# High and low parts of split fp32 weights, side by side instead of apart: a linear-attention and two-MoE kernel

## The chip, the cores and the metric

One core of a Trainium2 chip runs the whole program. The metric is the device time of one execution in microseconds, the median over several runs. Before the change it is 745.47 us (three runs).

## What is computed

A gated linear attention over 4 × 8 heads, 768 steps and 48 features a head; its output, 3072 tokens of 384 features, goes through two feed-forward layers: one with a softmax-weighted activation and a layer norm (1024 wide), one with h · cos(h) (2048 wide).

```python
def _attn_ref(q, k, v, alpha):
    for t in range(S):
        state = alpha[:, :, t, :, None] * state + np.einsum('bhd,bhe->bhde', k[:, :, t], v[:, :, t])
        y[:, :, t] = np.einsum('bhd,bhde->bhe', q[:, :, t], state)

def _moe_ref(x, w_in, w_out, g_ln):
    h = x @ w_in
    e = np.exp(h - np.max(h, axis=-1, keepdims=True))
    solu = h * (e / (np.sum(e, axis=-1, keepdims=True) + 1e-09))
    mu, var = np.mean(solu, axis=-1, keepdims=True), np.mean((solu - mu) ** 2, axis=-1, keepdims=True)
    return ((solu - mu) / np.sqrt(var + 1e-06) * g_ln) @ w_out

def _moe2_ref(x, w_in, w_out):
    h = x @ w_in
    return (h * np.cos(h)) @ w_out
```

The weights arrive as 64-bit floats and are turned into 32-bit ones on the chip.

## The kernel before

**Split products.** TensorE multiplies in a reduced fp32 form, F32R, at one column of the moving operand a cycle. To keep fp32 accuracy, each operand is split into a high part (a copy rounded to F32R, by ScalarE) and a low part (the difference, by VectorE or GpSimd), and each product is three matmuls: high·high, high·low, low·high. Every matmul has a load of its own, of 128 columns of weights in most cases, that runs beside the matmul ahead of it. The plain F32 matmuls and transposes of the attention are not split.

**Phase one** (about the first 340 us). The tokens come in 24 tiles of 128 (4 batches × 6 chunks). For each, attention forms `pa` (scores, L298), `px` (values, L329) and the state (`pst`, L348). Then `values_high` and `values_low` split its output into `xh` and `xl` (L380, L385), and `hidden` (L397) multiplies: here x is the loaded operand (the weights of TensorE) and `win_h`, `win_l` move, 512 columns at a time, 18 matmuls a tile. After softmax and norm, `turn` transposes the tile (L464: `so` is loaded, the identity moves, plain F32), `turn_high` and `turn_low` split it into `lth` and `ltl`, two tiles side by side, and `project` (L485 to L487) multiplies: `wout_h`, `wout_l` are loaded, `lth`, `ltl` move, 256 columns, 72 matmuls for each of 12 pairs of tiles. The result is `x2T`. The order of phase one is written out by hand as a list of words, PLAN; each word issues one step.

**Phase two.** The tokens come in 6 blocks (b) of 512, and the 2048 hidden features in 16 chunks (c) of 128. The 96 pairs (b, c) are slots in one sequence. `h2` (L573 to L575) makes a chunk's 9 matmuls: w2 is loaded, the block's `x2h`, `x2l` move, 512 columns. ScalarE and VectorE then form g = h · cos(h) and split it into `gh`, `gl` (L580 to L608). `out_mm` (L620 to L622) makes 9 matmuls for the chunk two slots back: w2 is loaded, `gh`, `gl` move. So a slot has 18 matmuls of 512 columns.

**Chunks of w2.** `w2load` fetches a chunk's 768 columns (384 for `h2`, 384 for `out_mm`) from HBM to `w2r`; `w2high` and `w2low` split it into `w2h` and `w2l` once (L550, L554), and all six blocks use the result. Chunks 0 to 3 are made in PLAN, 4 to 15 in the slots of block 0, three slots ahead. In each part the 128 columns of one load lie next to one another, 4 bytes apart, 512 bytes in all.

**Where things lie.** Tiles of a pool lie one behind the other in each partition. `x2h`, `x2l` of even blocks are in pool "q"; those of odd blocks are in pool "q3", behind `out`, a tile of ROWS columns of 4 bytes. In the built program `x2h` starts at byte 196576 of a partition in even blocks and at 128096 in odd ones: modulo 256, 224 and 96. `x2l` lies 6144 bytes on, at the same remainder. `w2h`, `w2l`, `gh`, `gl`, `xh`, `xl`, `win`, `wout`, `lth` and `ltl` all start at 224 modulo 256.

Of the kernel before, what the change touches and what calls it, by code (L numbers as in the profile page):

```python
# [27 lines left out]
DM = H * D  # L28
# [21 lines left out]
WB = 768  # L50
HB = WB // 2
NWB = ((KT * FF1 + NF1 * DM) // WB + NF2) * 2
ROWS = 96

TINY = float(np.array([897 << 20], np.int32).view(np.float32)[0])

# [65 lines left out]
def _build(tc, a):  # L122
# [5 lines left out]
    def flat(t):  # L128
        return t.rearrange("p a b -> p (a b)")

    with top:
# [22 lines left out]

        win_h = wi.tile([128, KT, FF1], F32R, name="win_h")
        win_l = wi.tile([128, KT, FF1], F32R, name="win_l")
        wout_h = wo.tile([128, NF1, DM], F32R, name="wout_h")
        wout_l = wo.tile([128, NF1, DM], F32R, name="wout_l")
        mask = at.tile([128, 128], F32, name="mask", bufs=1)
        d1p = at.tile([128, AW], F32, name="d1p", bufs=1)  # L160
        d1r = at.tile([128, AW], F32, name="d1r", bufs=1)
# [38 lines left out]
        def split(n):  # L200

            name = weights[n]
            w = T["w", name]
            j = int(name[1:])
            if name[0] == "o":
                for q in range(2):
                    ws = w[:, q * DM:(q + 1) * DM]
                    A.activation(ws, ws, AF.Copy, scale=gln[:, 2 * j + q:2 * j + q + 1])
                hi, lo = [t[:, 2 * j:2 * j + 2, :].rearrange("p a b -> p (a b)") for t in (wout_h, wout_l)]
            else:  # L210
                hi, lo = [flat(t)[:, j * 512:(j + 1) * 512] for t in (win_h, win_l)]
            A.activation(hi, w, AF.Copy)
            T["split", n] = hi, lo
# [161 lines left out]

        def values_high(i):
            px = T["px", i]
            xh = sm.tile([128, KT, 128], F32R, name=f"xh{i}", tag="xh", bufs=LA + 1)
            xl = sm.tile([128, KT, 128], F32R, name=f"xl{i}", tag="xl", bufs=LA + 1)
            A.activation(xh, px, AF.Copy, scale=2.0)  # L380
            T["x", i] = xh, xl

# [84 lines left out]
        def turn_high(i, half):  # L467
            g, j = i // GT, i % GT
            if ("lt", g) not in T:
                T["lt", g] = [sm.tile([128, NF1, GN], F32R, name=f"lt{x}{g}", tag="lt" + x) for x in "hl"]  # L470
            dst = (slice(None), slice(half * 4, half * 4 + 4), slice(j * C, (j + 1) * C))
            A.activation(T["lt", g][0][dst], T["pl", i, half], AF.Copy)

# [29 lines left out]

        def win_load(j):

            t = flat(sm.tile([128, NF1, GN], F32R, name=f"rawi{j}", tag="lth" if j % 2 else "ltl")).bitcast(F32)
            raw = t[:, 0:1024].bitcast(I32).rearrange("p (n two) -> p n two", two=2)
            top = mags[j % 2][:, j // 2 % 2 * 512:(j // 2 % 2 + 1) * 512]
            conv_load(a["win"][:, j * 512:(j + 1) * 512], f"i{j}",
                      (raw, (top.bitcast(I32), t[:, 1024:1536].bitcast(I32))))  # L510
# [32 lines left out]
        def w2load(c):  # L543
            raw = pools["q"].tile([128, WB], F32, name=f"w2r{c}", tag="w2r")
            SP.dma_start(raw, w2f[c])
            W[c] = raw, [pools["w"].tile([128, WB], F32R, name=f"w2{x}{c}") for x in "hl"]

        def w2high(c):
            raw, (wh, wl) = W[c]
            A.activation(wh, raw, AF.Copy)  # L550

        def w2low(c, eng=G):
            raw, (wh, wl) = W[c]
            eng.tensor_tensor(wl, raw, wh.bitcast(F32), ALU.subtract)  # L554
            W[c] = wh, wl

        def xhigh(b, k):
            if k == 0:
# [8 lines left out]
        def h2(b, c):  # L567
            xh, xl = X[b]
            wh, wl = W[c]
            ph = pools["h"].tile([128, BLK], F32, name=f"h2_{b}_{c}", tag="h2", bufs=3)  # L570
            for k in range(KT):
                ks = slice(k * 128, (k + 1) * 128)
                PE.matmul(ph, wh[:, ks], xh[:, k, :], start=k == 0, stop=False)  # L573
                PE.matmul(ph, wh[:, ks], xl[:, k, :], start=False, stop=False)  # L574
                PE.matmul(ph, wl[:, ks], xh[:, k, :], start=False, stop=k == KT - 1)  # L575
            Hs[b, c] = ph

        def turns(b, c):
# [32 lines left out]
        def out_mm(b, c):  # L611
            gh, gl = Gs.pop((b, c))
            wh, wl = W[c]
            if c == 0:
                O[b] = [pools["o"].tile([128, BLK], F32, name=f"o{b}_{f}", tag=f"o{f}", bufs=1 + (f < 2))
                        for f in range(KT)]
            for f in range(KT):
                fs = slice(DM + f * 128, DM + (f + 1) * 128)
                po = O[b][f]
                PE.matmul(po, wh[:, fs], gh, start=c == 0, stop=False)  # L620
                PE.matmul(po, wl[:, fs], gh, start=False, stop=False)  # L621
                PE.matmul(po, wh[:, fs], gl, start=False, stop=c == NF2 - 1)  # L622

        def out_end(b, fs=range(KT)):
            for f in fs:
# [323 lines left out]
```

## Time and profile before

| | us | share of the span |
|---|---|---|
| median of 3 runs | 745.47 | |
| profiled execution | 747.37 | |
| its span (first to last instruction) | 745.5 | |
| TensorE busy, matmuls | 721.9 | 97% |
| TensorE busy, weight loads (beside matmuls) | 608.6 | 82% |
| VectorE busy | 585.5 | 79% |
| ScalarE busy | 441.7 | 59% |
| GpSimd busy | 110.8 | 15% |

The busy time of a matmul in this profile reaches to a modelled end, past the start of the next one, so a busy TensorE can still have gaps between the starts of its matmuls that its columns don't explain. How far apart matmuls start is read from the timeline. PE is the engine's matmul row, PEld its row of weight loads; DVE is VectorE, ACT is ScalarE, POOL is GpSimd.

### The profile page before, as it was taken

The numbers are of one execution on the slowest core, as the hardware profiler recorded it, in microseconds if no ns is written. First come the engines' busy times: TensorE is split into PE (matmuls) and PEld (weight loads), VectorE is DVE, ScalarE is ACT, GpSimd is POOL, SyncE is SP. The second block draws the span as 40 slices with busy tenths as digits, with TensorE's granted clock in tenths as the row PEclk, the third lists the DMA queues.
The fourth block names the chain that finished last, engine by engine and source line by source line (L and its number), as shares of the span: only waits on it lengthen the run. The fifth ranks groups of instructions, "written<-read, shape, count | busy, mean of one in ns | idle before, by whom it ended". The sixth has DMA issues, their size and how long they took to land.

```text
span 745.5 us, 13977 instructions
## 1 busy us (share of the span) xinstructions
PE 721.9 (97%) x5580; PEld 608.6 (82%) x5580; DVE 585.5 (79%) x988; ACT 441.7 (59%) x771; POOL 110.8 (15%) x107
## 2 busy tenths in 40 slices
PE   6789999999999999999999999999999999999995
PEld 3578888899889898989888888888888888888884
DVE  6998988888698765543898878887888888888873
ACT  4799777866645556683665554555455555545442
POOL 3354531255311000310000000000000000000000
PEclk8899999999999999999999999999999999999999
DMA  9868777693433401111240421141142134134311
GB/s 324 233 175 202 246 199 215 209 257 95 91 78 59 89 2 44 29 59 40 87 125 32 148 72 50 44 140 36 49 135 63 43 99 137 41 91 143 89 38 48
DMA packets 27961, 81.19 MB, mean 109 GB/s; under 512 B 3600, under 2 KB 6928, under 8 KB 27888
## 3 DMA queue, kind: packets, MB, share of 16 engines
q1 hardware_dynamic: 27888, 80.22, 37.8%
q8 instruction: 46, 0.75, 0.4%
q14 instruction: 27, 0.22, 0.1%
HBM read 69.19 MB, written 11.01 MB: 108 GB/s over the span
## 4 chain that ended last, share of the span: by engine, by line
PE 55%; ACT 0%; DVE 0%; issue 0%
PE o L620 9%; PE h L575 9%; PE o L621 9%; PE h L573 9%; PE o L622 9%; PE h L574 9%; PE po L487 1%; PE po L486 1%; PE po L485 1%; PE pl L464 0%; ACT so L456 0%; ACT e L409 0%; DVE ob L632 0%; DVE ob L629 0%; ACT ob L630 0%; ACT c L451 0%
## 5 line engine op out<-in xcount | busy, mean ns | idle before, releaser
L593 ACT ACTIVATE g<-r,consts 128x512 f32<-128x512 f32 x96 | 69.5, 724 | 97.1 <-DVE r L587 97.1
L580 ACT ACTIVATE n<-h,consts 128x512 int32<-128x512 f32 x96 | 66.0, 688 | 86.0 <-PE h L575 86.0
L575 PE MATMUL h<-x2h,w2l 128*128 128x512 f32 x288 | 113.0, 392 | 0.0
L573 PE MATMUL h<-x2h,w2h 128*128 128x512 f32 x288 | 113.0, 392 | 0.0
L621 PE MATMUL o<-gh,w2l 128*128 128x512 f32 x288 | 112.7, 391 | 0.0
L620 PE MATMUL o<-gh,w2h 128*128 128x512 f32 x288 | 112.6, 391 | 0.0
L574 PE MATMUL h<-x2l,w2h 128*128 128x512 f32 x288 | 112.5, 391 | 0.0
L622 PE MATMUL o<-gl,w2h 128*128 128x512 f32 x288 | 112.1, 389 | 0.0
L586 DVE SCALAR_TENSOR_TENSOR r<-n,h 128x512 f32<-128x512 int32 x96 | 66.1, 688 | 40.1 <-ACT n L580 39.7
L598 DVE TENSOR_TENSOR g<-g,h 128x512 f32<-128x512 f32 x96 | 66.1, 688 | 24.4 <-ACT g L593 24.4
L485 PE MATMUL po<-lth,wout_h 128*128 128x256 f32 x288 | 83.1, 289 | 0.1
L486 PE MATMUL po<-ltl,wout_h 128*128 128x256 f32 x288 | 81.4, 283 | 0.0
L487 PE MATMUL po<-lth,wout_l 128*128 128x256 f32 x288 | 81.4, 283 | 0.0
L587 DVE SCALAR_TENSOR_TENSOR r<-n,r 128x512 f32<-128x512 int32 x96 | 66.5, 693 | 3.3
L608 DVE TENSOR_TENSOR gl<-g,gh 128x512 fp32r<-128x512 f32 x96 | 65.7, 684 | 1.5 <-ACT gh L603 1.5
L575 PEld LDWEIGHTS h<-x2h,w2l 128*128 128x128 f32 x288 | 54.0, 188 | 12.2
L620 PEld LDWEIGHTS o<-gh,w2h 128*128 128x128 f32 x288 | 54.0, 188 | 12.1 <-ACT x2T L491 0.2
L622 PEld LDWEIGHTS o<-gl,w2h 128*128 128x128 f32 x288 | 54.1, 188 | 11.8 <-DVE gl L608 0.2
L574 PEld LDWEIGHTS h<-x2l,w2h 128*128 128x128 f32 x288 | 54.0, 188 | 11.8
L621 PEld LDWEIGHTS o<-gh,w2l 128*128 128x128 f32 x288 | 54.1, 188 | 11.8
L573 PEld LDWEIGHTS h<-x2h,w2h 128*128 128x128 f32 x288 | 54.1, 188 | 11.5
L603 ACT ACTIVATE gh<-g 128x512 fp32r<-128x512 f32 x96 | 59.8, 623 | 2.0 <-DVE g L598 1.6
(115 smaller groups left out, 1371.3 us busy)
## 6 DMA issues: line engine op xcount, KB each, us to landing
raw<-w SPq DMA_DIRECT2D x16, 768.0 KB, 5.5
wraw<-w SPq DMA_DIRECT2D x32, 384.0 KB, 3.1
pk<-pack SPq DMA_DIRECT2D x42, 288.9 KB, 5.6
w2f<-top SPq DMA_DIRECT2D x16, 384.0 KB, 4.6
w2r<-w2f SPq DMA_DIRECT2D x16, 384.0 KB, 3.1
v<-vpack SPq DMA_DIRECT2D x24, 224.0 KB, 6.1
al<-alpha SPq DMA_DIRECT2D x18, 256.0 KB, 3.0
outT<-ob SPq DMA_DIRECT2D x18, 256.0 KB, 2.1
```

The lines of the kernel that those rows point to most:

```text
L485: PE.matmul(po, wout_h[:, k, fs], lh[:, k, :], start=k == 0, stop=False)
L486: PE.matmul(po, wout_h[:, k, fs], ll[:, k, :], start=False, stop=False)
L487: PE.matmul(po, wout_l[:, k, fs], lh[:, k, :], start=False, stop=k == NF1 - 1)
L573: PE.matmul(ph, wh[:, ks], xh[:, k, :], start=k == 0, stop=False)
L574: PE.matmul(ph, wh[:, ks], xl[:, k, :], start=False, stop=False)
L575: PE.matmul(ph, wl[:, ks], xh[:, k, :], start=False, stop=k == KT - 1)
L586: V.scalar_tensor_tensor(out=r, in0=n, scalar=-C1, in1=ph, op0=ALU.mult, op1=ALU.add)
L587: V.scalar_tensor_tensor(out=r, in0=n, scalar=-C2, in1=r, op0=ALU.mult, op1=ALU.add)
L593: A.activation(g, r, AF.Sin, bias=halfpi)
L620: PE.matmul(po, wh[:, fs], gh, start=c == 0, stop=False)
L621: PE.matmul(po, wl[:, fs], gh, start=False, stop=False)
L622: PE.matmul(po, wh[:, fs], gl, start=False, stop=c == NF2 - 1)
```

## The change

High and low parts that were two tiles become one, with the two parts of an element next to each other. A load of one part then reads every second element: its 128 columns lie 8 bytes apart and span 1024 bytes. This is done for wout, for x in phase one (`xh`, `xl`), and for chunks 7 to 11 of w2. In chunks 12 to 15 the high and low parts of two column groups are put together, so that columns lie 16 bytes apart and a load spans 2048 bytes. Chunks 0 to 6 stay at 4 bytes. The operations that write the parts write them at these steps.

Two places change. `out` has 128 columns instead of 96, so `x2h` of odd blocks starts at 128224, 224 modulo 256. `lth` and `ltl` get a pool of their own, "ltp", behind all others of phase one, and start at 64 modulo 256 instead of 224. Every other tile named above keeps 224 modulo 256; the low part of an interleaved tile starts 4 bytes behind the high one (8 bytes at step 16).

All engines carry the same operations in the same order as before, with the same numbers of partitions and elements; on ScalarE one wait (for the transfer of a w2 chunk) has become an instruction of its own. The new lines number three more than the old ones in phase one.

```diff
-ROWS = 96
+ROWS = 128
+STEPS = [1] * 7 + [2] * 5 + [4] * 4
...
+        ltp = left.enter_context(tc.tile_pool(name="ltp", bufs=2))
...
-        wout_h = wo.tile([128, NF1, DM], F32R, name="wout_h")
-        wout_l = wo.tile([128, NF1, DM], F32R, name="wout_l")
+        wout = wo.tile([128, NF1, DM, 2], F32R, name="wout")
+        wout_h, wout_l = wout[:, :, :, 0], wout[:, :, :, 1]
...
-                hi, lo = [t[:, 2 * j:2 * j + 2, :].rearrange("p a b -> p (a b)") for t in (wout_h, wout_l)]
+                both = wout[:, 2 * j:2 * j + 2].rearrange("p a b two -> p (a b) two")
+                hi, lo = both[:, :, 0], both[:, :, 1]
...
-            xh = sm.tile([128, KT, 128], F32R, name=f"xh{i}", tag="xh", bufs=LA + 1)
-            xl = sm.tile([128, KT, 128], F32R, name=f"xl{i}", tag="xl", bufs=LA + 1)
+            x = sm.tile([128, KT, 128, 2], F32R, name=f"x{i}", tag="x", bufs=LA + 1)
+            xh, xl = x[:, :, :, 0], x[:, :, :, 1]
...
-                T["lt", g] = [sm.tile([128, NF1, GN], F32R, name=f"lt{x}{g}", tag="lt" + x) for x in "hl"]
+                T["lt", g] = [ltp.tile([128, NF1, GN], F32R, name=f"lt{x}{g}", tag="lt" + x) for x in "hl"]
...
-            W[c] = raw, [pools["w"].tile([128, WB], F32R, name=f"w2{x}{c}") for x in "hl"]
+            step = STEPS[c]
+            if step == 1:
+                t = pools["w"].tile([128, 2, 6, 128], F32R, name=f"w2hl{c}")
+                whole = [t[:, x] for x in range(2)]
+            elif step == 2:
+                t = pools["w"].tile([128, 6, 128, 2], F32R, name=f"w2hl{c}")
+                whole = [t[:, :, :, x] for x in range(2)]
+            else:
+                t = pools["w"].tile([128, 3, 128, 2, 2], F32R, name=f"w2hl{c}")
+                whole = [t[:, :, :, :, x].rearrange("p a f b -> p a b f") for x in range(2)]
+            W[c] = raw, whole, step
...
-                PE.matmul(ph, wh[:, ks], xh[:, k, :], start=k == 0, stop=False)
-                PE.matmul(ph, wh[:, ks], xl[:, k, :], start=False, stop=False)
-                PE.matmul(ph, wl[:, ks], xh[:, k, :], start=False, stop=k == KT - 1)
+                PE.matmul(ph, wh(k), xh[:, k, :], start=k == 0, stop=False)
+                PE.matmul(ph, wh(k), xl[:, k, :], start=False, stop=False)
+                PE.matmul(ph, wl(k), xh[:, k, :], start=False, stop=k == KT - 1)
```

`wh(j)` and `wl(j)` are the 128 columns of group j (0 to 2 for `h2`, 3 to 5 for `out_mm`) at the chunk's step.

## Rows read from the trace of the kernel before

**Rows 1.** The page: busy us (share) and instructions; granted clock in 40 slices.
```profile
PE 721.9 (97%) x5580; PEld 608.6 (82%) x5580; DVE 585.5 (79%) x988; ACT 441.7 (59%) x771; POOL 110.8 (15%) x107
...
PEclk8899999999999999999999999999999999999999
```
**Rows 2.** Timeline of PE, an even block (b = 2), one slot: start us, us, what.
```profile
502.08 0.39 PE L573 MATMUL h<-x2h,w2h 128*128 128x512 f32 x1
...
506.16 0.39 PE L573 MATMUL h<-x2h,w2h 128*128 128x512 f32 x1
```
**Rows 3.** Timeline of PE, an odd block (b = 1), one slot.
```profile
423.68 0.40 PE L573 MATMUL h<-x2h,w2h 128*128 128x512 f32 x1
...
427.84 0.40 PE L573 MATMUL h<-x2h,w2h 128*128 128x512 f32 x1
```
**Rows 4.** Timeline of PE, phase one, matmuls with wout, 21 starts apart.
```profile
325.68 0.28 PE L487 MATMUL po<-lth,wout_l 128*128 128x256 f32 x1
...
328.20 0.28 PE L487 MATMUL po<-lth,wout_l 128*128 128x256 f32 x1
```
**Rows 5.** Timeline of PE, phase one, eight transposes in a row.
```profile
336.14 1.04 PE L464 MATMUL pl<-ident,so 128*128 128x128 f32 x8
```
**Rows 6.** Groups by line and shape: count, busy us, mean ns, idle before.
```profile
L485 PE MATMUL po<-lth,wout_h 128*128 128x256 f32 x288 | 83.1, 289 | 0.1
...
L573 PEld LDWEIGHTS h<-x2h,w2h 128*128 128x128 f32 x288 | 54.1, 188 | 11.5
...
L397 PE MATMUL ph<-win_l,xh 128*128 128x512 f32 x144 | 45.4, 396 | 1.9 <-DVE win_l L218 1.9
...
L464 PE MATMUL pl<-ident,so 128*128 128x128 f32 x192 | 25.5, 274 | 0.6 <-ACT so L456 0.6
...
L348 PE MATMUL pst<-v,kt 128*32 128x64 f32 x640 | 12.5, 221 | 2.2 <-ACT kt L305 2.2
...
L348 PEld LDWEIGHTS pst<-v,kt 128*32 128x32 f32 x640 | 10.3, 110 | 4.8 <-ACT kt L305 3.6 <-issue 0.5 <-ACT xh L380 0.4
```
**Rows 7.** Busy time by stage: blocks b = 1 and b = 2 whole.
```profile
core 0: us, PE busy (x) PEld busy (x) DVE busy (x) ACT busy (x) POOL busy (x), PEclk, DMA share, GB/s
402.87:469.43 66.56, 66.56 (x289) 54.04 (x288) 53.87 (x100) 33.92 (x54) 4.68 (x7) 1.00 0.25 76
469.43:534.71 65.28, 65.28 (x289) 54.05 (x288) 53.82 (x100) 33.94 (x54) 4.31 (x7) 1.00 0.24 77
```
**Rows 8.** Timeline of PE, phase one, one state update.
```profile
252.20 0.63 PE L348 MATMUL pst<-v,kt 128*32 128x64 f32 x32
```
**Rows 9.** Busy time by stage: 40 to 160 us, all engines.
```profile
40.00:160.00 120.00, 116.70 (x1454) 102.63 (x1455) 106.30 (x163) 101.28 (x184) 47.74 (x37) 1.00 0.76 218
```
**Rows 10.** Busy time of L397 alone, then of L485 alone, until 160 us.
```profile
0.00:160.00 160.00, 46.79 (x184) 0.96 0.78 229
...
0.00:160.00 160.00, 27.85 (x96) 0.96 0.78 229
```
**Rows 11.** Groups by line: operations with and without steps, ScalarE and VectorE.
```profile
L655 DVE SCALAR_TENSOR_TENSOR wup<-wup,wraw 128x384 f32<-128x384 uint32 x48 | 26.8, 559 | 1.7
...
L190 ACT ACTIVATE low<-raw 128x768 bf16<-128x768 f32 x16 | 17.4, 1086 | 6.2 <-POOL top L198 3.7 <-DVE top L198 2.4
...
L385 DVE SCALAR_TENSOR_TENSOR xl<-px,xh 128x384 fp32r<-128x384 f32 x24 | 13.3, 553 | 2.9 <-ACT xh L380 2.7
...
L550 ACT ACTIVATE w2h<-w2r 128x768 fp32r<-128x768 f32 x16 | 13.3, 836 | 4.4 <-DMA w2r<-w2f 4.4
```

More of the change, by code (lines that the diff above doesn't have):

```diff
@@ L504, in win_load @@
         def win_load(j):
-            t = flat(sm.tile([128, NF1, GN], F32R, name=f"rawi{j}", tag="lth" if j % 2 else "ltl")).bitcast(F32)
+            t = flat(ltp.tile([128, NF1, GN], F32R, name=f"rawi{j}", tag="lth" if j % 2 else "ltl")).bitcast(F32)
             raw = t[:, 0:1024].bitcast(I32).rearrange("p (n two) -> p n two", two=2)
@@ L545, in w2load @@
             SP.dma_start(raw, w2f[c])
-            W[c] = raw, [pools["w"].tile([128, WB], F32R, name=f"w2{x}{c}") for x in "hl"]
+            step = STEPS[c]
[9 more added lines that the diff above has]
+            W[c] = raw, whole, step
         def w2high(c):
-            raw, (wh, wl) = W[c]
-            A.activation(wh, raw, AF.Copy)
+            raw, (wh, wl), step = W[c]
+            A.activation(wh, raw.rearrange("p (a b f) -> p a b f", a=3, b=2) if step == 4 else
+                         raw.rearrange("p (j f) -> p j f", j=6), AF.Copy)
         def w2low(c, eng=G):
-            raw, (wh, wl) = W[c]
-            eng.tensor_tensor(wl, raw, wh.bitcast(F32), ALU.subtract)
-            W[c] = wh, wl
+            raw, (wh, wl), step = W[c]
+            eng.tensor_tensor(wl, raw.rearrange("p (a b f) -> p a b f", a=3, b=2) if step == 4 else
+                              raw.rearrange("p (j f) -> p j f", j=6), wh.bitcast(F32), ALU.subtract)
+            W[c] = [(lambda j, t=t: t[:, j // 2, j % 2]) if step == 4 else (lambda j, t=t: t[:, j]) for t in (wh, wl)]
         def xhigh(b, k):
@@ L571, in h2 @@
             for k in range(KT):
-                ks = slice(k * 128, (k + 1) * 128)
-                PE.matmul(ph, wh[:, ks], xh[:, k, :], start=k == 0, stop=False)
-                PE.matmul(ph, wh[:, ks], xl[:, k, :], start=False, stop=False)
-                PE.matmul(ph, wl[:, ks], xh[:, k, :], start=False, stop=k == KT - 1)
+                PE.matmul(ph, wh(k), xh[:, k, :], start=k == 0, stop=False)
+                PE.matmul(ph, wh(k), xl[:, k, :], start=False, stop=False)
+                PE.matmul(ph, wl(k), xh[:, k, :], start=False, stop=k == KT - 1)
             Hs[b, c] = ph
@@ L617, in out_mm @@
             for f in range(KT):
-                fs = slice(DM + f * 128, DM + (f + 1) * 128)
                 po = O[b][f]
-                PE.matmul(po, wh[:, fs], gh, start=c == 0, stop=False)
-                PE.matmul(po, wl[:, fs], gh, start=False, stop=False)
-                PE.matmul(po, wh[:, fs], gl, start=False, stop=c == NF2 - 1)
+                PE.matmul(po, wh(KT + f), gh, start=c == 0, stop=False)
+                PE.matmul(po, wl(KT + f), gh, start=False, stop=False)
+                PE.matmul(po, wh(KT + f), gl, start=False, stop=c == NF2 - 1)
         def out_end(b, fs=range(KT)):
```

## The prediction

> **What bounds the kernel now.** I read the page's busy shares first, then the granted clock, the table by stage, and the starts of single matmuls. TensorE is busy 97% of the span, VectorE 79%, ScalarE 59%, and the granted clock stands at 9 tenths or more, its upper level of 2.4 GHz, from the third of 40 slices on [rows 1]. So time goes only where a matmul starts later after the one before it than its columns need. A "pitch" below is that distance from start to start; the trace's own durations of matmuls (389 ns) overlap and say less.
>
> Four pitches carry the argument.
> - A 512-column F32R matmul of an even block: 18 in 506.16 − 502.08 = 4.08 us, 226.7 ns each [rows 2]. Its columns need 512 / 2.4 = 213.3 ns.
> - The same in an odd block: 18 in 427.84 − 423.68 = 4.16 us, 231.1 ns [rows 3].
> - A 256-column one of phase one: 21 in 328.20 − 325.68 = 2.52 us, 120.0 ns each; the columns need 106.7 [rows 4].
> - A transpose of 128 plain F32 columns: 8 in 1.04 us, the last with a duration of 0.274, so (1.04 − 0.274) / 7 = 109 ns [rows 5, 6].
>
> So each F32R matmul carries about 13.3 ns beyond its columns, whether it has 512 or 256 of them: it goes with the load that runs beside each matmul, not with the columns.
>
> Is it reading that collides? Whole blocks answer: 66.56 us for an odd block, 65.28 for an even one, with the same count of matmuls and VectorE and ScalarE equally busy [rows 7]. They differ only in where the moving x2 lies: in the built program it starts at byte 128096 of a partition in odd blocks (96 modulo 256) and at 196576 in even ones (224 modulo 256, as do all w2 tiles and g). An address cannot matter to a cost that is fixed; so at least part of the excess is the moving operand and the weights getting in each other's way.
>
> The speeds of the two reads: a load of 128 columns takes 188 ns, one of 32 takes 110, so (188 − 110) / 96 = 0.81 ns a column, 4 bytes each [rows 6]. An F32R moving column passes in 0.417 ns, so now the moving read runs through memory twice as fast as the weights. Plain F32 moves at half that speed: the 32 records of a state update, four at a time with 64 columns each, take (0.63 − 0.221) / 7.75 = 0.053 us a group, 0.82 ns a column [rows 6, 8]. In a transpose, then, both reads walk at the same speed, and there the excess is 109 − 106.7 = 2.3 ns instead of 13.3, though a full 128-column load runs beside each. This pair is what I build on: **equal walking speed goes with almost no excess**. A step of 8 bytes makes the weights walk 8 bytes in 0.81 ns, the moving read 4 in 0.417: equal.
>
> **The change, part by part** (against the profiled 747.37; the median 745.47 is 1.9 less, and I subtract from it).
> - Nothing is added on TensorE, VectorE, GpSimd or SyncE, and the order is the same; one wait of ScalarE, for the transfer of a w2 chunk that its split reads, stands as an instruction of its own ahead of that split; what is queued behind it was behind the split before. Addresses and steps change.
> - Odd x2 moves by 128 bytes to 224 modulo 256, where even x2 lies: 3 odd blocks × (66.56 − 65.28) = **−3.8**. Bounds: 0 if the stepped chunks ask for another place, −3.8.
> - wout at step 8: 288 × 3 = 864 matmuls of 256 columns [rows 6], from 120.0 to 106.7 + 2.3 = 109.0: −9.5. Below, no gain; above, +13.3 each if a load that spans twice the memory collides twice as often, +11.5. lt also moves, to 64 modulo 256; no row shows that offset. I take the row nearest, the transpose: **−9.5**.
> - x of phase one at step 8: 3 × 144 = 432 matmuls [rows 6], from 226.7 to 213.3 + 2.3 = 215.6: **−4.8** (bounds −4.8, +5.8).
> - w2 chunks 7 to 11 at step 8: 5 chunks × 6 blocks × 18 = 540 matmuls × 11.1: **−6.0** (bounds −6.0, +7.2).
> - w2 chunks 12 to 15 at step 16: 432 matmuls. The weights now walk twice as fast as the moving read, the mirror of today; no row shows it. Bounds: −4.8 (all the excess goes), and 4 times the memory, +13.3 × 3 × 432 = +17.3. Halfway between all and nothing: **−2.4**.
> - Not all of phase one's gain arrives. In 40 to 160 us VectorE is busy 106.3 of 120 us beside TensorE's 116.7 [rows 9]; 184 of the hidden matmuls and 96 × 3 of wout's lie before 160 [rows 10], 2.0 + 3.2 = 5.2 us of gain. When TensorE runs ahead, VectorE's keys, masks and scans are late next. I take half as lost: **+2.6** (bounds 0, 5.2).
> - Splitting into stepped tiles: ScalarE writes w2, wout and x at 8 or 16 bytes, VectorE and GpSimd read and write so. Nearest rows: ScalarE reading at 8 bytes and writing at 4 takes 1086 ns for 768 elements against 836 unstepped; VectorE reading at 8 bytes 559 for 384 against 553 [rows 11]. So at most 0.25 us for each of 13 ScalarE splits of 768 and half of it for 24 of 384: 6.3 us in all. ScalarE has the room (59% of the span; 101.3 of 120 us even in 40 to 160 [rows 9]), so 0; without that cover up to 6.
>
> [...]
>
> Sum: −3.8 − 9.5 − 4.8 − 6.0 − 2.4 + 2.6 = −23.9, so 745.5 − 23.9 = 721.6; rounded **721.5** (the profiled one 723.4). Its own range: with step 16 between 0 and −4.8 and phase one losing 5.2 to 0, 726.6 to 716.6, say 716 to 728.
>
> **Rivals.**
> - *Only the move counts.* The 13.3 ns is a fixed turn-round from load to matmul in F32R, and only the odd blocks' 4.4 ns more is a collision. For it: 512 and 256 columns carry the same 13.3. Against: the transposes, with the same loads, don't. 745.5 − 3.8 = **741.6**.
> - *Half.* Equal speed locks the two reads together, but sometimes in the wrong phase: lt and wout lie 96 bytes apart, x2 and w2 don't. Half of the steps' 20.1 plus the move: 745.5 − 13.9 = **731.6**.
> - *The steps cost (the other side).* What collides is counted by the memory that a load spans: 512 bytes now, 1024 at step 8, 2048 at step 16. Then the 11 ns of a load comes once more at step 8 and three times more at 16: 9.5 + 4.8 + 6.0 + 432 × 33.3 = 34.7, less 3.8: **776.4**. It decides (2% slower) from (14.9 + 3.8) / 2268 stepped matmuls = 8.3 ns each. For it: that address matters at all. Against: equal speed in the transposes.
> - *Loads at step 16 no longer hide.* A load's 128 columns take 104 ns of the 227; beyond 2.2 times that it bounds the chunk. At 3 times, 311 ns: 432 × (311 − 227) = 36.3; with the other parts at −21.5, 745.5 + 14.8 = **760.3**. No row speaks for or against it.
> - *Reads never collide*: **745.5**. Rows 7 speak against it.
>
> [...]
>
> **How the numbers follow.** Chances: my forecast 0.52; half 0.11; only the move 0.16; no collisions 0.03; the steps cost 0.12; step-16 loads exposed 0.06. About 2% (14.9 us) is what a measurement of this kernel can tell from no change: faster than 730.6 holds my forecast, 0.52; within 2% the next three, 0.30; slower 0.18. The range 715 to 746 holds the forecast with its bounds and the three within 2%, 0.82, and leaves out the two slower ones. The likeliest case alone: 716 to 728.
>
> **What the profile after would show.** The starts of wout's matmuls 109 ns apart, hidden's and those of chunks 7 to 11 215 to 216; chunks 0 to 6 still 226.7, now in odd blocks too; an unstepped odd block's chunk 4.08 us instead of 4.16. Blocks 1 to 4 equal in time, each 65.28 − 90 × 0.0111 = 64.3 us, less up to 72 × 0.0111 = 0.8 for step 16: 63.5 to 64.3. TensorE's waits in 40 to 160 us grow by a few us. I am wrong if stepped pitches stay at 226.7 (only the move), exceed it (the steps cost), or if only chunks 12 to 15 do (loads exposed; then the load itself is longer than 188 ns).

## The result, and the profile after

| | before | after |
|---|---|---|
| median, us | 746.35 (4 runs beside those of after: 744.67, 745.47, 747.22 and 804.35) | 755.89 (4 runs, 754.72 to 757.29) |
| ratio | | 1.0126, 95% interval 1.0105 to 1.0147 |
| profiled execution, us | 747.37 | 754.92 |
| its span, us | 745.5 | 753.1 |

One of the four runs of before, of 804.35 us, was a slow one that the ratio leaves out. By the ratio the change costs 0.0126 × 746 = 9.4 us. The forecast was 721.5 us, with a range of 715 to 746. The loss is less than the 2% that was set as the bound for "slower", but its interval lies clear of no change.

The page of after has these lines: busy time by engine, the granted clock, the chain that ended last by line, and the costliest groups (name, count | busy us, mean ns | idle before).

```profile
PE 730.0 (97%) x5580; PEld 635.6 (84%) x5580; DVE 587.3 (78%) x988; ACT 445.3 (59%) x771; POOL 113.0 (15%) x107
...
PEclk8799999999999999999999999999999999999999
...
PE o L635 8%; PE o L633 8%; PE h L588 8%; PE h L587 8%; PE o L634 8%; PE h L589 8%; DVE w2hl L568 1%; ACT w2hl L563 1%; PE po L489 1%; PE po L488 1%; PE po L490 1%; DVE r L600 0%; ACT g L607 0%; DVE r L601 0%; PE pl L467 0%; ACT x2h L576 0%
...
L587 PEld LDWEIGHTS h<-x2h,w2hl 128*128 128x128 f32 x288 | 63.3, 220 | 8.8
```

Against [rows 1], the number of matmuls and loads is the same and the granted clock still stands at 9 tenths or more from the third slice on. The loads' busy time rose by 27 us, as their mean duration in `h2` went from 188 ns [rows 6] to 220. And the splits of w2 (`w2hl`, lines 563 and 568) have come into the chain that ends last, with 1% each.

The table by stage says where the time went. Its stretches are the blocks b = 0, 1 and 2 of after (us, busy time by engine with counts, granted clock, DMA share, GB/s):

```profile
322.97:409.12 86.15, 82.88 (x432) 72.44 (x431) 61.02 (x88) 53.33 (x83) 1.36 (x2) 1.00 0.21 66
409.12:475.70 66.58, 66.58 (x290) 57.94 (x288) 53.81 (x100) 33.95 (x54) 4.32 (x7) 1.00 0.25 76
475.70:542.29 66.59, 66.59 (x289) 57.95 (x288) 53.80 (x100) 33.94 (x54) 4.32 (x7) 1.00 0.24 75
```

And block 0 of before, which the groups ahead of the prediction don't show:

```profile
321.68:402.88 81.20, 80.59 (x433) 69.49 (x431) 58.67 (x88) 50.62 (x84) 1.40 (x3) 1.00 0.23 70
```

Phase two begins 1.3 us later (322.97 against 321.68). Block 0 takes 4.95 us more. Odd blocks keep their 66.56 us [rows 7], and even blocks rise from 65.28 to 66.59, to the length of odd ones. So the blocks are equal in time now, but at the slower level. Block 5, an odd one, takes 0.2 us more (675.48 to 746.54 us against 666.56 to 737.40), and what lies behind the last matmul 1.5 us less in this profile: 1.3 + 4.95 + 2 × 1.31 + 0.2 − 1.5 = 7.6 us, the difference of the spans of these two executions (over all runs the ratio gives 9.4).

Inside block 2 of after, single starts of `h2` and `out_mm` show three levels of pitch (the distance from the start of one matmul to the next). In each pair below the first row is a chunk's first `h2` matmul and the second the start of `out_mm`, nine matmuls later: chunk 5 (4 bytes), chunk 10 (8 bytes), chunk 14 (16 bytes).

```profile
496.35 0.39 PE L587 MATMUL h<-x2h,w2hl 128*128 128x512 f32 x1
498.39 0.39 PE L633 MATMUL o<-gh,w2hl 128*128 128x512 f32 x1
...
517.01 0.39 PE L587 MATMUL h<-x2h,w2hl 128*128 128x512 f32 x1
519.11 0.39 PE L633 MATMUL o<-gh,w2hl 128*128 128x512 f32 x1
...
533.84 0.40 PE L587 MATMUL h<-x2h,w2hl 128*128 128x512 f32 x1
535.95 0.40 PE L633 MATMUL o<-gh,w2hl 128*128 128x512 f32 x1
```

That is 2.04 / 9 = 226.7 ns at 4 bytes, 2.10 / 9 = 233.3 at 8, and 2.11 / 9 = 234.4 at 16. The forecast had 215.6 at 8 bytes.

In phase one, wout's matmuls stayed as they were in [rows 4], and those of `hidden` became slower (timeline of TensorE; the two rows of the first fence are 21 starts apart; in the second, where one row holds several matmuls, 12):

```profile
332.01 0.28 PE L490 MATMUL po<-lth,wout 128*128 128x256 f32 x1
...
334.53 0.28 PE L490 MATMUL po<-lth,wout 128*128 128x256 f32 x1
```

```profile
296.18 1.09 PE L400 MATMUL ph<-win_h,x 128*128 128x512 f32 x4
...
298.98 0.63 PE L400 MATMUL ph<-win_h,x 128*128 128x512 f32 x2
```

Wout: 2.52 / 21 = 120.0 ns, as before. `hidden`: 2.80 / 12 = 233.3 ns, where the prediction took 226.7 as its level and 215.6 as the new one.

The extra of block 0 is another matter: there TensorE waits. The first fence has ScalarE's and VectorE's splits of a chunk at 8 bytes (starts 377.04 and 377.98) and of one at 16 (387.28 and 388.91), what follows the latter on VectorE, and the next splits at 16 bytes. The second has TensorE at the same place: the starts of three slots, and the wait between.

```profile
377.04 0.91 ACT L563 ACTIVATE w2hl<-w2r 128x768 fp32r<-128x768 f32 x1
...
387.28 1.60 ACT L563 ACTIVATE w2hl<-w2r 128x768 fp32r<-128x768 f32 x1
...
392.52 1.59 ACT L563 ACTIVATE w2hl<-w2r 128x768 fp32r<-128x768 f32 x1
...
397.76 1.59 ACT L563 ACTIVATE w2hl<-w2r 128x768 fp32r<-128x768 f32 x1
...
377.98 0.96 DVE L568 TENSOR_TENSOR w2hl<-w2r,w2hl 128x768 fp32r<-128x768 f32 x1
...
388.91 1.59 DVE L568 TENSOR_TENSOR w2hl<-w2r,w2hl 128x768 fp32r<-128x768 f32 x1 [0.73 <-ACT w2hl L563]
390.40 0.67 DVE L600 SCALAR_TENSOR_TENSOR r<-n,h 128x512 f32<-128x512 int32 x1
...
391.72 0.68 DVE L622 TENSOR_TENSOR gl<-g,gh 128x512 fp32r<-128x512 f32 x1
...
394.14 1.60 DVE L568 TENSOR_TENSOR w2hl<-w2r,w2hl 128x768 fp32r<-128x768 f32 x1 [0.81 <-ACT w2hl L563]
```

```profile
383.91 0.39 PE L587 MATMUL h<-x2h,w2hl 128*128 128x512 f32 x1
...
388.43 0.40 PE L587 MATMUL h<-x2h,w2hl 128*128 128x512 f32 x1
...
392.46 0.51 PE L635 MATMUL o<-gl,w2hl 128*128 128x512 f32 x1 [1.29 <-DVE gl L622]
...
394.20 0.40 PE L587 MATMUL h<-x2h,w2hl 128*128 128x512 f32 x1
...
404.89 0.40 PE L587 MATMUL h<-x2h,w2hl 128*128 128x512 f32 x1
```

ScalarE's split of 768 elements takes 1.60 us at 16 bytes where it took 0.836 unstepped [rows 11]; VectorE's takes 1.59 where it took 0.96 even at 8 bytes. VectorE waits for ScalarE, then splits for 1.59 us, and only then does the r, r and `gl` that `out_mm` needs: TensorE waits 1.29 us at 392.46. The two engines wait for each other in a round: ScalarE's split (392.52), VectorE's split of the same chunk (394.14) and its r and r, then ScalarE's g, which reads r, and ScalarE's next split (397.76). One round takes 5.24 us, more than the 4.20 us of a slot without a wait. A slot of 18 × 233.3 ns = 4.20 us takes 5.77 here (388.43 to 394.20). The four slots in which a chunk is split at 16 bytes, from 383.91 to 404.89, take 20.98 us where 4 × 4.20 = 16.8 would do: block 0 stalls by 4.2 us, once.

### The profile page after: what moved, and what is told of

Read it like the earlier page. It is cut to its first block, busy times and chain, and to the rows that moved or that the text cites. A ratio compares the mean times of both kernels' runs of the same rounds, so it can differ in the third digit from the quotient of the medians.

```text
span 753.1 us, 13978 instructions
## 1 busy us (share of the span) xinstructions
PE 730.0 (97%) x5580; PEld 635.6 (84%) x5580; DVE 587.3 (78%) x988; ACT 445.3 (59%) x771; POOL 113.0 (15%) x107
## 4 chain that ended last, share of the span: by engine, by line
PE 52%; DVE 2%; ACT 2%; issue 0%; ACTq 0%; DVEq 0%
PE o L635 8%; PE o L633 8%; PE h L588 8%; PE h L587 8%; PE o L634 8%; PE h L589 8%; DVE w2hl L568 1%; ACT w2hl L563 1%; PE po L489 1%; PE po L488 1%; PE po L490 1%; DVE r L600 0%; ACT g L607 0%; DVE r L601 0%; PE pl L467 0%; ACT x2h L576 0%
## 5 line engine op out<-in xcount | busy, mean ns | idle before, releaser
L635 PE MATMUL o<-gl,w2hl 128*128 128x512 f32 x288 | 113.7, 395 | 2.9 <-DVE gl L622 2.9
L633 PE MATMUL o<-gh,w2hl 128*128 128x512 f32 x288 | 113.5, 394 | 0.0
L588 PE MATMUL h<-x2l,w2hl 128*128 128x512 f32 x288 | 113.4, 394 | 0.0
L587 PE MATMUL h<-x2h,w2hl 128*128 128x512 f32 x288 | 113.4, 394 | 0.0
L589 PE MATMUL h<-x2h,w2hl 128*128 128x512 f32 x288 | 113.1, 393 | 0.0
L634 PE MATMUL o<-gh,w2hl 128*128 128x512 f32 x288 | 113.1, 393 | 0.0
L400 PE MATMUL ph<-win_h,x 128*128 128x512 f32 x288 | 86.6, 403 | 1.2 <-DVE so L429 1.1
L488 PE MATMUL po<-lth,wout 128*128 128x256 f32 x288 | 83.3, 289 | 0.0
L489 PE MATMUL po<-ltl,wout 128*128 128x256 f32 x288 | 81.6, 283 | 0.0
L490 PE MATMUL po<-lth,wout 128*128 128x256 f32 x288 | 81.5, 283 | 0.0
L635 PEld LDWEIGHTS o<-gl,w2hl 128*128 128x128 f32 x288 | 63.3, 220 | 13.1 <-DVE gl L622 4.5
L587 PEld LDWEIGHTS h<-x2h,w2hl 128*128 128x128 f32 x288 | 63.3, 220 | 8.8
L589 PEld LDWEIGHTS h<-x2h,w2hl 128*128 128x128 f32 x288 | 63.3, 220 | 8.8
L633 PEld LDWEIGHTS o<-gh,w2hl 128*128 128x128 f32 x288 | 63.4, 220 | 8.5 <-ACT x2T L494 0.2
L634 PEld LDWEIGHTS o<-gh,w2hl 128*128 128x128 f32 x288 | 63.3, 220 | 8.4
```

Of the source, the lines that this page charges most:

```text
L400: PE.matmul(ph[:, n * 512:(n + 1) * 512], xs[:, k, :], w[:, k, n * 512:(n + 1) * 512], start=k == 0 and xs is xh and w is win_h, stop=k == ...
L488: PE.matmul(po, wout_h[:, k, fs], lh[:, k, :], start=k == 0, stop=False)
L489: PE.matmul(po, wout_h[:, k, fs], ll[:, k, :], start=False, stop=False)
L490: PE.matmul(po, wout_l[:, k, fs], lh[:, k, :], start=False, stop=k == NF1 - 1)
L587: PE.matmul(ph, wh(k), xh[:, k, :], start=k == 0, stop=False)
L588: PE.matmul(ph, wh(k), xl[:, k, :], start=False, stop=False)
```

## The experiments

Times of experiments stand against runs of the kernel before on the same chip. "Distance" below is the start of the moving operand minus the start of the weights, modulo 256 bytes; before, it is 0 in even blocks, for g, for `hidden` and for wout, and 128 for x2 of odd blocks. In the kernels that scan or that run a bench, time is no comparison: rows of matmuls stand behind the program, each row 24 matmuls with a load of its own, into a tile that nothing reads.

**e1: the move alone.**

```diff
-ROWS = 96
+ROWS = 128
```

> The kernel before with one edit: odd x2 starts at 224 modulo 256, like even x2. All theories: an odd block takes 65.28 us instead of 66.56, every pitch of the six blocks 226.7 ns, and the time falls by 3 x 1.28 = 3.8 us, ratio 0.995. If the odd blocks' excess had another cause (their pool's other tiles), they stay at 66.56 us and the ratio is 1.000.

Measured: 742.09 us against 745.83, ratio 0.9940 (0.9922 to 0.9959). The odd block 1 now takes what even ones take, 65.28 us:

```profile
403.06:468.34 65.28, 65.28 (x289) 54.07 (x288) 53.83 (x100) 33.94 (x54) 4.48 (x7) 1.00 0.24 77
```

The term −3.8 of the prediction was right (measured −4.5, interval −5.8 to −3.1). Everything else in the change then costs some 13.9 us together, and the next three runs share that out.

**e4: the kernel after without steps in w2; wout and x stepped, lt moved, x2 moved.**

```diff
-STEPS = [1] * 7 + [2] * 5 + [4] * 4
+STEPS = [1] * 16
```

> The changed kernel with all chunks of w2 at 4 bytes; wout and x of phase one stay at 8 bytes, odd x2 moved, lt in its own pool. If the pitch of w2's chunks and the slow 16-byte splits of block 0 are what the change costs: block 0 back to 81.2 us, blocks 1 to 5 at 65.3, phase one 1.3 us longer than before, together 745.5 + 1.3 - 3.8 = 743.0, ratio 0.997. If phase one's steps cost more than the 1.3 us seen in where phase two begins, the ratio is over 1.000.

Measured: 744.01 us, ratio 0.9969 (0.9956 to 0.9983). Blocks 1 to 4 take 65.28 us, as in e1. So, against e1, phase one's part of the change costs 0.0029 × 746 = 2.2 us (give or take 1.7) where 9.5 + 4.8 − 2.6 = 11.7 was to be gained.

**e7: e1 and wout stepped, nothing else.**

```diff
-        wout_h = wo.tile([128, NF1, DM], F32R, name="wout_h")
-        wout_l = wo.tile([128, NF1, DM], F32R, name="wout_l")
+        wout = wo.tile([128, NF1, DM, 2], F32R, name="wout")
+        wout_h, wout_l = wout[:, :, :, 0], wout[:, :, :, 1]
...
```

> The kernel with odd x2 moved, and wout at 8 bytes; x and w2 at 4 bytes, lt where it was (224 modulo 256). If x of phase one at 8 bytes is what cost phase one its 1.9 us (hidden at 233 instead of 227) and wout nothing: hidden back at 227, wout's pitch 120, the time equal to that with odd x2 moved alone, 742.1. If lt's own place kept wout's pitch at 120: wout's pitch here is about 127 (256 columns and 20 ns), 864 x 6.7 ns = 5.8 us more, 747.9.

Measured: 742.81 us, ratio 0.9965 (0.9949 to 0.9982); wout's median pitch 120 ns, `hidden`'s 227. This cannot be told from e1, so wout's step is worth nothing either way. What is left for phase one's 2.2 us is x, whose 432 matmuls × (233.3 − 226.7) would be 2.9 us (and lt at another place, at the same 120 ns). The start of phase two says the same, though it varies by some us between profiles: 322.97, 324.45 and 326.15 in the three kernels with x stepped (after, e4, e6), 321.68, 322.19 and 322.70 in those without (before, e1, e7).

**e6: the kernel after without 16 bytes** (the last four chunks at 8).

```diff
-STEPS = [1] * 7 + [2] * 5 + [4] * 4
+STEPS = [1] * 7 + [2] * 9
```

> The changed kernel with chunks 12 to 15 at 8 bytes as chunks 7 to 11 are. If 16-byte writing of the parts (ScalarE 1.59 us, VectorE 1.59 against 0.89 and 0.96) stalls block 0: its waits vanish and it takes 81.2 + 162 x 0.0067 = 82.3 us instead of 86.1; pitch of chunks 12 to 15 goes from 234.5 to 233.3, 0.5 us over six blocks. Together 4.3 us less than the changed kernel, 751.5. If the stall of block 0 had another cause: 755.

Measured: 750.04 us against 745.36, ratio 1.0061 (1.0039 to 1.0083). Blocks 0 and 2 in the table by stage:

```profile
326.15:407.92 81.77, 81.60 (x432) 70.29 (x431) 58.43 (x88) 50.89 (x83) 1.17 (x2) 1.00 0.23 70
474.32:540.71 66.39, 66.39 (x290) 54.92 (x288) 53.79 (x100) 33.94 (x54) 4.50 (x7) 1.00 0.24 76
```

Block 0 is down from 86.15 to 81.77 us, and TensorE waits for no `gl` any more: the stall was the splits at 16 bytes. The other blocks are only 0.2 us shorter than in after, so 16 bytes beside 8 cost the matmuls little. The ratios of the four kernels make one chain: move −0.0060, phase one +0.0029, nine chunks at 8 bytes +0.0092, 16 in place of 8 +0.0065; of 746 us, −4.5 + 2.2 + 6.9 + 4.8 = 9.4, each of the last three give or take about 2. The third has a check of its own: 9 chunks × 6 blocks × 18 × 6.7 ns = 6.5 us.

**e2: all of w2 at 4 bytes, and x2 and g of each block at another distance.** This and e3 ask whether equal speed or the address decides.

```diff
...
+DX = [0, 32, 64, 96, 160, 192]
+DG = [0, 32, 64, 96, 160, 192]
...
+                X[b] = [pools["q3" if b % 2 else "q"].tile([128, KT * BLK + PAD], F32R, name=f"x2{x}{b}", tag="x2" + x, bufs=1)
+                        [:, DX[b] // 4:DX[b] // 4 + KT * BLK].rearrange("p (k n) -> p k n", k=KT) for x in "hl"]
...
```

> All loads at 4 bytes. The moving x2 and g of block b start D bytes behind the place where moving operand and weights agree modulo 256: D = 0, 32, 64, 96, 160, 192 for b = 0 to 5. Theory A (where the two reads stand to each other decides): the pitches of the blocks differ, between 226.7 ns (D = 0) and at least the 231 to 233 known at D = 128, some offsets perhaps below 226.7, down to 215.6; every matmul of a block has settled at its block's value. Theory B (a load costs by the memory that it spans, and the odd blocks of before were a special place): 226.7 ns in every block.

Measured, median pitch by block: 226.7, 233.3, 228.9, 233.3, 234.3, 233.4 ns. Blocks 1, 2 and 4 (distance 32, 64, 160):

```profile
402.73:469.90 67.17, 67.17 (x290) 53.99 (x288) 53.88 (x100) 33.99 (x54) 4.61 (x7) 1.00 0.23 75
469.90:535.90 66.00, 66.00 (x290) 54.08 (x289) 53.78 (x100) 33.96 (x54) 4.31 (x7) 1.00 0.24 76
...
603.04:670.52 67.48, 67.48 (x290) 54.23 (x288) 55.52 (x107) 33.98 (x54) 0.00 (x0) 1.00 0.30 88
```

Against 65.28 us at distance 0 (e1): the address of x2 and g alone moves a block by 0.7 to 2.2 us, with the loads' busy time unchanged at 54 us.

**e3: the kernel after with all of w2 at 8 bytes, distances 0, 32, 64, 96, 128, 160** (set as in e2).

```diff
-STEPS = [1] * 7 + [2] * 5 + [4] * 4
+STEPS = [2] * 16
...
```

> The changed kernel with all 16 chunks of w2 at a step of 8 bytes; the moving x2 and g of block b start D = 0, 32, 64, 96, 128, 160 bytes behind agreement modulo 256, b = 0 to 5. Theory A (equal speed locks the reads, and the offset decides whether they are locked onto or off each other): 233.3 ns at D = 0 as in chunks 7 to 11 of the changed kernel, and at some other D a pitch below 226.7, at best 215.6. Theory B (8-byte loads cost by the memory that they span): 233 ns or more at every D.

Measured: 235.6, 233.3, 233.4, 233.3, 231.4, 233.3 ns. Blocks 1 and 4:

```profile
406.99:474.21 67.22, 67.22 (x290) 56.66 (x288) 53.79 (x100) 33.99 (x54) 4.29 (x7) 1.00 0.24 75
...
608.61:675.29 66.68, 66.68 (x289) 56.35 (x288) 55.43 (x107) 33.92 (x54) 0.00 (x0) 1.00 0.30 89
```

At none of the six distances do 8 bytes bring a pitch near 215; even the best block is slower than the plain 226.7. For F32R, equal speed as a cure is refuted at these distances, and e5 has 16. What the step did was to give up the place at distance 0: at 4 bytes the same matmuls are 226.7 there and 229 to 234 at the other distances of e2; at 8 bytes they are 231 to 236 at all six.

**e5: the same in a bench, finer, and where 109 ns came from.**

```diff
+            def row(step, d, n=BLK, cols=128, reps=24):
+                for _ in range(reps):
+                    PE.matmul(sink[:cols, :n], wt[:, 0:cols * step:step], xm[:, d:d + n], start=True, stop=True)
...
```

> The kernel with odd x2 moved, and behind its last output matmul rows of 24 equal matmuls into a tile that nothing reads; the time is meaningless. Loads of 128 columns at 4, 8, 16 bytes beside 512 moving F32R columns, moving operand D = 0 to 240 bytes (by 16) behind agreement modulo 256. Theory B (a load costs about 20 ns at every step and offset, and D = 0 at 4 bytes is the one place where the reads fall into step with each other): 4 bytes 226.7 at D = 0, 229 at 64, 233 to 235 elsewhere; 8 bytes 231 to 236 everywhere; 16 bytes 234 to 235. Theory A (some offset at 8 or 16 bytes is free of collisions): one or more rows at 215 to 222. With 32, 64 and 96 loaded columns: 218 to 220, 223 and 228 if each loaded column costs its share of 20 ns, 233 if the cost is fixed. Transposes with loads at 8 and 16 bytes: 109 if it is the slower moving read that hides the load there; above 109 if equal walking speed did.

Rows of 512 columns, first 4 bytes at distance 0 and 32, then 8 bytes at 0 and 192, then 16 bytes at 0 (start us, us from the first start to the modelled end of the last):

```profile
734.24 5.15 PE L679 MATMUL sink<-x2h,w2h 128*128 128x512 f32 x22
...
745.24 5.06 PE L679 MATMUL sink<-x2h,w2h 128*128 128x512 f32 x21
...
823.29 5.06 PE L679 MATMUL sink<-x2h,w2h 128*128 128x512 f32 x21
...
890.33 4.99 PE L679 MATMUL sink<-x2h,w2h 128*128 128x512 f32 x21
...
912.62 5.10 PE L679 MATMUL sink<-x2h,w2h 128*128 128x512 f32 x21
```

Less 0.39 for the last one and divided by the count less one: 226.7, 233.5, 233.5, 230.0 and 235.5 ns. Other pitches of bench rows in the text are means over the last 15 of the 23 intervals between a row's starts, when it has settled. Over all 16 distances by 16 bytes, the rows at 4 bytes have 226.6 to 234.7, those at 8 bytes 229.8 to 234.1, those at 16 bytes 233.3 to 240.4. The scans' values return to 0.2 ns (64: 228.9 both times).

And the rows on which the 109 is tested: 128 F32R columns beside a load at 4 bytes and at 8, 256 beside one at 16, and transposes with the loaded operand at 4, at 8 and at 16 bytes.

```profile
1036.49 2.17 PE L679 MATMUL sink<-x2h,w2h 128*128 128x128 f32 x18
...
1041.63 2.64 PE L679 MATMUL sink<-x2h,w2h 128*128 128x128 f32 x21
...
1072.54 5.06 PE L679 MATMUL sink<-x2h,w2h 128*128 128x256 f32 x21
...
1083.84 2.24 PE L694 MATMUL sink<-ident,x2T 128*128 128x128 f32 x19
...
1091.73 2.44 PE L694 MATMUL sink<-ident,x2T 128*128 128x128 f32 x19
...
1106.15 2.32 PE L694 MATMUL sink<-ident,x2T 128*128 128x128 f32 x18
```

By single starts in the trace, the first row's matmuls stand 111.5 ns apart and the second's 117.7, though the columns of both need only 128 × 0.417 = 53 ns; the third's 233.3, where the columns need 106.7. (Pitches of 512 and 256 columns differ by 226.7 − 120.0 = 106.7 ns [rows 2, 4], so an F32R column takes 0.417 ns. The 2.4 of the prediction is this rate, in columns a ns.) The columns fill half of these paces or less, and the pace moves with the step of the load, so here the loads set it: about 111 ns for one at 4 bytes, 118 at 8, 233 at 16.

Transposes are 109.2 ns apart at 4 bytes, at each of three distances, and 120.0 at 8. Their columns are the same in both, so what is loaded has a part in their pace, and the two values lie near those of F32R loads. But at 16 bytes transposes stay at 120.0 to 121.2 ns (last row), where the F32R row has 233.3. That a transpose is paced by its load alone is therefore argued and not shown. By the sign that was given ahead of the run, "above 109 if equal walking speed did", the transposes even speak for equal speed within plain F32: 120.0 is 13.3 over their columns' 106.7 (an estimate: 128 at half the speed of F32R, about the 0.82 ns a column of [rows 6, 8]). What no row supports is the use of that rule on F32R, where 8 bytes gave 229.8 to 234.1 instead of 215.6. The granted clock was 1.00 in these stretches; some rows between 1047 and 1064 us, where it was 0.58 on the mean, are left out.

**e8: which address counts.** The same bench; the weights are shifted and the moving operand stays, then both are shifted alike, then fewer columns.

```diff
+            for e in range(0, 64, 4):
+                row(1, 0, e=e)
+            for d in (4, 8, 16, 32, 48):
+                row(1, d, e=d)
...
```

> As the rows of matmuls behind the program before (its time is meaningless), now telling which place matters. First 16 rows: moving operand fixed at 224 modulo 256, the loaded weights start e = 0 to 240 bytes (by 16) later, 4-byte steps. Theory R (the distance between the two reads decides): 226.7 at e = 0 and e = 16 (the mirror of D = 240), 229 at e = 192, 231 to 235 elsewhere. Theory P (the moving operand's own place decides, whatever the weights do): 226.7 in all 16. Next 5 rows: both moved by the same 16 to 192 bytes: R gives 226.7, P gives the values seen before for D = 16 (231.5), 32 (233.3), 64 (228.9), 128 (232.9), 192 (233.5). With 480 to 320 moving columns: the excess over the columns' time stays 13.3 ns at D = 0 and 20 at D = 32 if it goes with the load. 256 columns over all D at 4 and 8 bytes: 4 bytes between 117 and 127, 8 bytes 119 to 121; a D below 120.0 at 4 bytes would be a better place for lt.

Weights shifted by 16 and by 32 bytes, which makes distances of 240 and 224:

```profile
740.64 5.15 PE L678 MATMUL sink<-x2h,w2h 128*128 128x512 f32 x22
...
746.09 5.06 PE L678 MATMUL sink<-x2h,w2h 128*128 128x512 f32 x21
```

226.7 and 233.5 ns, and e5 has 226.7 and 233.4 at these distances: the weights' address matters as much as the moving operand's. With both shifted by 16, 32, 64, 128 and 192 bytes: 230.1, 226.9, 226.7, 227.3, 227.3, four of five within 0.6 ns of distance 0. So it is mostly the distance. Not all of it: weights shifted by 240 (distance 16) gave 226.7 where e5 had 231.5 at that distance. Rows of 256 columns at 4 bytes had 120.0 at distance 0 and one low pair, 113.3 at distances 112 and 192; at 8 bytes 117.8 to 121.1 at all 16. With fewer moving columns the place stops mattering: at distances 0 and 32, 480 columns take 216.6 and 220.1 ns and 448 columns 202.7 and 206.7, but 384 take 173.3 at both and 320 take 146.7 at both, 13.3 over their columns.

**e10: all 64 distances by 4 bytes, to see whether a place below 226.7 exists.**

```diff
+            for d in range(64):
+                row(1, d)
...
```

> A bench behind the kernel before, whose time means nothing: rows of 24 matmuls, each with a load of its own at 4 bytes, moving operand shifted against the weights. First 512 columns at all 64 distances from 0 to 252 by 4 bytes; then 256 columns at distances 108, 116, 188 and 196; then 256 columns with 64 columns loaded, 16 distances. Distance decides: 226.7 at 0 and near it (252, 240), 229 at 64 and 12, 231 to 236.6 elsewhere, as the coarse rows had it. If there is a place below 226.7 (the 256-column rows had one at 113.3 where the usual is 117 to 120), it shows as a row of 220 or less, and x2, g and phase one's win belong there: 1,584 + 432 matmuls and more by 6.7 ns. If the rows repeat to 0.1 ns with those of the coarse bench, distance alone sets them; if they scatter by some ns at the same distance, the phase at which a row begins has a part.

Distances 20 and 28:

```profile
761.63 4.96 PE L678 MATMUL sink<-x2h,w2h 128*128 128x512 f32 x20
...
772.99 5.15 PE L678 MATMUL sink<-x2h,w2h 128*128 128x512 f32 x22
```

240 and 226.7 ns. No place lies below 226.7: seven of 64 stand there (0, 28, 60, 156, 236, 240, 252), the others between 228 and 240. For 512 columns and loads at 4 bytes the kernel before already had the best place in even blocks, and e1 has it in all. The rows at the 16 distances of e5 return within 0.7 ns. But distance 244 had 240.0 here and 233.3 in e8, and 248 had 230.1 and 233.3: distance decides most of it, and something else has a part. In rows of 256 columns, distances 108, 116, 188 and 196 gave 120.0, 121.6, 115.5 and 119.7 ns; with only 64 columns loaded, 16 distances gave 113.3 to 119.7.

**e9: e1, and lt moved against wout to distance 192.**

```diff
...
+        ltp = left.enter_context(tc.tile_pool(name="ltp", bufs=2))
...
+        ltp.tile([128, 24], F32, name="gap", bufs=1)
...
```

> The kernel before with out at 128 columns (odd x2 moved) and one more edit: lth and ltl in a pool of their own with a gap of 96 bytes ahead, so that they start at 160 modulo 256 while wout stays at 224: the distance from weights to moving operand goes from 0 to 192. All weights at 4 bytes. Distance decides for 256 columns too: the row of 256 columns at distance 192 was 113.3 ns in the bench, against 120.0 at 0, so the 864 matmuls with wout go from 120.0 to about 113.3 and the program from 742.1 to 742.1 - 864 x 6.7 / 1000 = 736.3 us, or a microsecond or two more where phase one waits for something else. Rival, phase one is not set by these matmuls (the transposes and splits ahead of them are late): pitch 113 but 741 to 742. Rival, the bench's 113.3 was a matter of its row (one weight tile, one moving tile) and not of the distance: pitch stays 120 and the time stays 742.

Measured: 740.36 us, ratio 0.9929 (0.9911 to 0.9947). Phase two begins at 318.42 us, 3.8 before e1's and before that of any other kernel here. The pitch of wout's matmuls has two levels. Two stretches of the timeline, nine starts and then 21 apart:

```profile
299.73 0.28 PE L488 MATMUL po<-lth,wout_l 128*128 128x256 f32 x1
...
300.75 0.28 PE L488 MATMUL po<-lth,wout_l 128*128 128x256 f32 x1
...
305.20 0.28 PE L488 MATMUL po<-lth,wout_l 128*128 128x256 f32 x1
...
307.67 0.28 PE L488 MATMUL po<-lth,wout_l 128*128 128x256 f32 x1
```

1.02 / 9 = 113.3 ns, the bench's value, and 2.47 / 21 = 117.6 (117.8 by single starts). By the median of its starts, each of the 36 runs of 24 matmuls (one output group of a pair) is at one level or the other, 16 at the lower and 20 at the higher, all at the same distance; the mean is 116. So the miss is one of size: the expected 736.3 took the low level for all. The kernel is 0.5% to 0.9% faster than before. Its interval overlaps with that of e1: what this move adds is seen in the trace of phase one, and the times don't tell it from nothing.

## Why the prediction was wrong, point by point

- **Odd x2 to 224 modulo 256: right.** −3.8 forecast, −4.5 measured (e1). In after, too, the unstepped chunks 3 to 6 of odd blocks stand at 226.7 in `h2`. In odd blocks of before, `h2` had 232.8 and `out_mm` 229.4, though only the operands of `h2` lay at distance 128: a slow place next to it cost `out_mm` some ns as well.
- **The step that failed: "equal walking speed goes with almost no excess", carried over to F32R.** It rested on one pair, the transposes' 109 ns against 106.7 of columns [rows 5, 6]. I read 2.3 ns as a collision that had all but gone. On F32R matmuls the rule does not hold: at 8 bytes, where the two speeds were to be equal, 512 columns take 229.8 to 234.1 ns at each of 16 distances (e5) and 256 columns 117.8 to 121.1 (e8), not 215.6 and 109.0. And 109 ns is less than an F32R load needs: F32R matmuls of 128 columns, which pass in 53 ns, are 111.5 apart at 4 bytes and 117.7 at 8 (e5). It is likely that a transpose's columns and its load happen to take about the same time, and then its small excess says nothing on collisions; but the transposes at 16 bytes, at 120, do not fit F32R's 233, so the cause of their 109 stays open. A number that comes out near the columns' time was taken for the columns' time, and the other thing that could set it, the load, was not held against it. The rows ahead of the prediction did give a load's pace, 0.81 ns a column, 104 ns for 128; it was used for the speed of reading, and as a bound only for step 16.
- **wout, −9.5: 0 measured (e7).** 109 ns could not be reached. At 8 bytes the load alone needs 118 to 119 ns (e5), more than the columns' 106.7. The pitch stayed at 120.0.
- **x of phase one, −4.8, and chunks 7 to 11, −6.0: the sign was wrong.** 226.7 became 233.3 instead of 215.6. For x the price is 2.2 us, give or take 1.7 (e4 against e1), for the five chunks 540 × 6.7 ns = 3.6. The bounds given for them, +5.8 and +7.2, contain this, but the range did not reach to them.
- **Chunks 12 to 15, −2.4: wrong in sign too.** 234.4 ns on the matmuls, 432 × 7.7 = 3.3 us. By e5 the load at 16 bytes sets a pace of 233 ns alone. That agrees with the rival "loads no longer hide" in kind, though chunks at 8 bytes stand at 233.3 too and the rows can't tell a load that no longer hides from a collision. The rival's price was put at 311 ns a load, and 311 ns is indeed what the trace gives as a load's duration (310), but loads overlap, and from start to start it is 233.
- **Splits at 0 (bounds 0 to 6): wrong.** They cost 4.2 us, all at 16 bytes. I took the nearest row, a read at 8 bytes, and the cover of the whole span, 59%. In block 0 ScalarE and VectorE pass each chunk from one to the other, and a slot holds 4.20 us; a round of two splits of 1.6 us with r, r and g behind them takes 5.24. The time of a split at 16 bytes could not be had from a row at 8: the traces of before and after give 0.836 us unstepped and 0.89 at 8 bytes on ScalarE, 0.96 for both on VectorE, and 1.6 on both engines at 16 bytes. A load's duration goes the same way (188, 193 to 196 and 310 ns), the pitch of a matmul beside a load does not: 8 bytes already cost 6.7 ns at distance 0, and 16 bytes 2 more (e5: 226.7, 233.5 and 235.5).
- **+2.6 of gain lost in phase one** had nothing to apply to.
- **The rivals.** "Only the move counts", 741.6, gives the time of e1, not of after. "Half", 731.6, falls with the rule that it halves: no distance tried at 8 bytes brought a gain. "The steps cost", 776.4, was right in sign (the 8.3 ns a matmul from which it is 2% slower is 8.2: 18.7 us / 2268); its mechanism, a price by the memory that a load spans, was not: in e5 8 bytes are no worse than 4 at an ordinary distance (233.5 ns at 8 bytes and distance 0, 233.5 at 4 bytes and distance 32), and 16 cost about 3 ns more (16 rows of 24 take 89.3 us at 8 bytes and 90.6 at 16). "Reads never collide" falls by e2, e5 and e10, as the prediction said from [rows 7]: pitch goes from 226.7 to 240 by address alone. That it is the reads that collide is inferred from this; no run looks into them.
- **What the profile was to show.** Blocks 1 to 4 equal in time: they are, at 66.6 us instead of 63.5 to 64.3. Chunks 0 to 6 at 226.7: in `h2`, chunks 3 to 6 are; 0 to 2 have 228 to 231 right behind the chunks at 16 bytes, and 227.1 to 227.6 in e6, which has none. The sign of being wrong, stepped pitches over 226.7, came.

In one sentence: the address effect was read rightly from odd and even blocks, and then widened to a rule about speed that one coincidence seemed to support; the steps kept 1,404 matmuls of 512 columns (432 of x, 540 and 432 of w2) off the lowest pitch, which they have without steps at distance 0, and got nothing for it.

What stays open is why the distance modulo 256 matters, why one distance can have two levels, and what sets the 109 and 120 ns of transposes. No run here looks into the reads themselves. The best kernels found are e1 and e9, both faster than the two compared: 0.9940 and 0.9929.

## What to carry to other kernels

Before an operation's time is taken as evidence on one resource, hold it against every other thing that could set it: here a bench row with fewer columns would have told that an F32R load alone needs 111 ns. Where a load at 4 bytes runs beside each F32R matmul of 512 columns, try moving operand and weights at the same address modulo 256 before any change of layout (here 226.7 ns, and up to 240 at other distances in e10). And price a strided write by the engine that does the writing in the stage where it runs, with the work handed between engines there, not by its busy share over the span (here 1.6 us for each of two splits at 16 bytes, and a round of 5.24 us against a slot of 4.20).

## What the runs showed of the hardware

- An F32R matmul of 512 columns with a load beside it at 4 bytes starts 226.7 to 240 ns after the one before (e10), for the most part by the distance of its two operands modulo 256; the columns need 213.3 (an estimate: 512 at the 0.417 ns of [rows 2, 4]). Steps of 4, 8 and 16 bytes have lowest levels of 226.7, 229.8 and 233.3 (e5).
- With 512 columns the excess does not shrink with the columns that are loaded: at distance 0, loads of 32, 64 and 96 columns gave 231.6, 229.3 and 229.9 ns, more than 226.7 with 128 (e5). With 256 columns at distance 0 it does: 113.3 with 64 loaded (e10), 120.0 with 128 (e8).
- An F32R load of 128 columns sets a pace of 111 to 112 ns at 4 bytes, 118 to 119 at 8, and 233 at 16, though its duration in the trace is 188 to 192, 193 to 198 and 308 to 329; durations of loads overlap and are no bound (e5; durations also in before and after).
- Transposes of 128 plain F32 columns are 109.2 ns apart with the loaded operand at 4 bytes, 120.0 at 8, and 120.0 to 121.2 at 16, not 233 (e5).
- At one and the same distance (192, 256 columns) runs of 24 matmuls stand at one of two levels, 113.3 or 117.8 ns (e9).
- ScalarE and VectorE take 0.836 and 0.96 us for a split of 768 elements written 4 bytes apart, 0.89 and 0.96 at 8 bytes, and 1.6 each at 16 (before and after; VectorE reads one of its two operands at the same step).
